# Compact keys and queries, 64-row score products, float32r halves for part of the softmax weights, float32r token transposes

## The chip, the cores and the metric

The kernel runs on one core of one Trainium2 chip. The metric is device time in microseconds (us) of one execution: the median of several runs. A profiled execution gives the trace. In the profile PE is TensorE's matmul queue, PEld its weight loads, DVE VectorE, ACT ScalarE, POOL GpSimd, SP SyncE, which issues most DMAs.

## What is computed

Attention with capped scores over 8 batches, 12 heads, 448 tokens and a head size of 64, and behind it a mixture of 8 experts over the 3584 tokens (model width 768, hidden width 1024):

```python
scores = scale * np.matmul(q, k.transpose(0, 1, 3, 2))
scores = cap * np.tanh(scores / cap)
attn = np.exp(scores - np.max(scores, axis=-1, keepdims=True))
attn = attn / (np.sum(attn, axis=-1, keepdims=True) + 1e-09)
attn_out = np.matmul(attn, v)                 # heads side by side: x, [3584, 768]
...
logits = x @ w_gate + modality_bias[modality_id]
e_idx = np.argmax(logits, axis=1)             # one expert per token
h = np.maximum(x[mask] @ w1[e], 0.0)
out[mask] = gate_w[mask, None] * (h @ w2[e])
```

All inputs and outputs are float32. A product in float32 takes two TensorE instructions, each with its own weight load. float32r is a four-byte type that TensorE multiplies in one instruction; since it keeps fewer bits, the kernel splits a float32 tensor into a float32r high part (a cast) and a float32r rest (a subtract), and adds the products high x high, high x low and low x high.

## The kernel before

**Attention** (`attention`, line 420) runs over 48 head pairs g, two heads j of one batch each, in four steps a pair. Keys lie in units of 128: three of each head (units 0 to 5), and a seventh unit that holds the last 64 keys of both heads. `prep` (line 491), called in step 1 for the next pair, loads keys and queries (`load_qk`, line 383; each head's 64 rows stand twice, in rows 0 to 63 and 64 to 127) and splits them: `kh` is the high part of the keys; `qs` holds the queries' high part in its upper 64 rows and the rest in its lower 64, so that one product over 128 rows with `kh` gives high x high plus high x low; `kl` is the keys' rest. `scores` (line 532) computes two units a step, one in the last: two products of 448 queries for a unit, three for the seventh, into PSUM tile `sc` (line 547); then ACT takes the tanh (line 552) and the exponential (line 553), which gives the softmax weights `pt`, with keys on the rows and queries on the columns.

`weigh` (line 555) runs one pair later: step c multiplies 112 queries of the pair before (the columns of `pt` as stationary weights) with the values `va` as moving columns, 64 values, 8 gate logits and a column of ones a head (73), all in float32: one product for the seventh unit of both heads (line 558, 146 columns) and six of 73 (line 567). After every second step `normalize` (line 575) divides `po` by the column of sums on DVE. In each step PE's order is: the scores of pair g, then the weighing of pair g - 1. The values' gate columns come from small products (`later_gate`, line 461, and `gate_values`, line 395, for the first three pairs, whose line 403 is the only place where outputs of 64 columns are written to halves of the array).

**Experts** (`run_slots`, line 836): slots of 384 tokens of one expert, then shorter ones of 256 or 128 (`ENDS`). A slot gathers its tokens into `xg` (line 716), turns 128 x 128 blocks with TensorE transposes (line 752), splits them, multiplies with `w1` (lines 776 to 780) and `w2` (line 802), each as three float32r products, and scatters the rows. The weights pass through a ring of `nstage` = 4 raw buffers (`load_raw`, line 723, on SP's queue) and are split by ACT (line 732) and DVE (line 733). Short slots use 256 or 512 moving columns for the high weights (line 779) and 128 or 256 for the low ones (line 780).

Of the kernel before, what the change touches and what calls it, by code (L numbers as in the profile page):

```python
# [28 lines left out]
F32 = mybir.dt.float32  # L30
F32R = mybir.dt.float32r
# [3 lines left out]
ALU = mybir.AluOpType  # L35
# [8 lines left out]
VA = D + E + 1  # L44
KU, KR = 3, 64
NU = 2 * KU + 2
KW = 2 * S + KR
OWN = KU * 128
GE = 2 * E
# [15 lines left out]
class Program:  # L65
    def __init__(self, tc, qT, kT, v, vT, cap, mod, wgb, mb, w1, w2, out):
        self.tc, self.nc = tc, tc.nc
        self.qT, self.kT, self.v, self.vT = qT, kT, v, vT
        self.cap, self.mod, self.wgb, self.mb = cap, mod, wgb, mb
        self.w1, self.w2, self.out = w1, w2, out  # L70
# [17 lines left out]
    def constants(self, cpool, dram):  # L88
# [6 lines left out]
        make_identity(nc, self.ident)  # L95
        self.capt = cpool.tile([128, 1], F32, name="capt")
# [286 lines left out]
    def load_qk(self, pool, g, parts=1):  # L383
        nc = self.nc
        b, hp = divmod(g, NP)
        kr = pool.tile([128, 2, S], F32, name="kr")
        qr = pool.tile([128, 2, S], F32, name="qr")
        step = 2 * S // parts
        for i in range(parts):
            cs = slice(i * step, (i + 1) * step)  # L390
            for t, src in ((kr, self.kT), (qr, self.qT)):
                self.load(t.rearrange("p j s -> p (j s)")[:, cs], src[b, hp][:, cs])
        return kr, qr
# [26 lines left out]
    def attention(self, qk, first):  # L420
        tc, nc = self.tc, self.nc
        with ExitStack() as st:
# [11 lines left out]
            khs, kls, kds = [], [], []  # L434
            for i in range(2):
                kh = kp.tile([128, KW], F32R, name=f"kh{i}")
                kl = kp.tile([128, 2, OWN], F32R, name=f"kl{i}")
                kd = kp.tile([128, 2, KR], F32R, name=f"kd{i}")
                nc.gpsimd.memset(kh.bitcast(F32)[:, S : S + KR], 0.0)
                nc.gpsimd.memset(kd.bitcast(F32), 0.0)  # L440
                khs.append(kh)
                kls.append(kl)
                kds.append(kd)
# [47 lines left out]
            def prep(g):  # L491
                b, hp = divmod(g, NP)
                kr, qr = first if g == 0 else self.load_qk(qk, g)
# [3 lines left out]
                kh, kl, kd = khs[g % 2], kls[g % 2], kds[g % 2]  # L497
                qs = sp.tile([128, 2, S], F32R, name="qs")
                qd = sp.tile([128, S], F32R, name="qd")
                keep = self.pin if g < 2 else (lambda inst: inst)  # L500

                copy = (lambda out, in_: keep(nc.scalar.copy(out, in_) if g == 0 else nc.vector.tensor_copy(out, in_)))
                for jj in ((0, 1),) if g else ((0,), (1,)):
                    js = slice(jj[0], jj[-1] + 1)
                    for j in jj:
                        o = j * (S + KR)
                        keep(nc.vector.tensor_copy(kh[:, o : o + S], kr[:, j]))
                    copy(qs[:, js], qr[:, js])
                    keep(nc.vector.tensor_tensor(qs[D:, js], qr[D:, js], qs[D:, js], op=ALU.subtract))  # L509
                    for j in jj:  # L510
                        o, r = j * (S + KR + KR), j * KR
                        keep(nc.vector.tensor_tensor(kl[:, j], kr[:, j, r : r + OWN], kh[:, o : o + OWN], op=ALU.subtract))
                for j in range(2):
                    rows = slice(j * D, (j + 1) * D)
                    r, o = OWN * (1 - j), (OWN, S + KR)[j]
                    copy(qd[rows], qr[rows, j])
                    keep(nc.vector.tensor_tensor(
                        kd[rows, j], kr[rows, j, r : r + KR], kh[rows, o : o + KR], op=ALU.subtract
                    ))
                return qs, qd, kh, kl, kd, va  # L520

            def gate_of(g, va, vt=None):
# [5 lines left out]
                self.put_gate_values(va, vg)  # L528

            GROUPS = ((0, 1), (2, 3), (4, 5), (6,))  # L530

            def scores(step, pt, qs, qd, kh, kl, kd):
                units = GROUPS[step]
                sc = ps_s.tile([128, 2, 512], F32, name="sc")
                for i, u in enumerate(units):
                    if u < 2 * KU:
                        j, c = divmod(u, KU)
                        o = j * (S + 2 * KR) + c * 128
                        todo = [(kh[:, o : o + 128], qs[:, j]), (kl[:, j, c * 128 : (c + 1) * 128], qs[:, j])]
                    else:  # L540
                        todo = [
                            (kh[:, OWN : OWN + 128], qs[:, 0]),
                            (kh[:, S : S + 128], qs[:, 1]),
                            (kd.rearrange("p j s -> p (j s)"), qd),
                        ]
                    for n, (k, q) in enumerate(todo):
                        move = nc.tensor.matmul(sc[:, i, :S], k, q, start=n == 0, stop=n == len(todo) - 1)  # L547
# [3 lines left out]
                n = len(units)  # L551
# [523 lines left out]
```

## Time and profile before

| | us |
|---|---|
| time before, median of 3 runs (lowest to highest) | 1001.65 (1001.46 to 1002.1) |
| the profiled execution's own time | 1003.47 |
| its span, first to last instruction | 1001.9 |
| mean granted TensorE clock | 0.992 of full speed |
| attention, about | 0 to 475 |
| experts, about | 475 to 1002 |

A row of the timeline reads: start, length, engine, line, operation, out<-in, shapes, count; instructions of one kind that follow each other are merged into a row, whose length is from the first start to the last end. A row of a group reads: line, engine, operation, out<-in, shapes, count, then busy us and the mean ns of one, then idle time before them. `128*112 128x73` is a product with stationary weights of 128 rows and 112 columns and 73 moving columns. The trace names float32r operands of TensorE f32 as well.

### The profile page before, as it was taken

What the parts mean: (1) busy time and instruction counts of PE and PEld (TensorE: products, weight loads), DVE (VectorE), ACT (ScalarE), POOL (GpSimd) and SP (SyncE); (2) the same over time, 40 slices, a digit from 0 to 9 for tenths busy, and PEclk for the clock granted to TensorE, in tenths of its full rate; (3) what the DMA queues carried; (4) which work ended last, traced back from release to release, by engine and by line L of the source; (5) the groups of instructions that cost most, each with busy time, mean ns of one, the idle gap of its engine ahead of it and who ended that gap; (6) DMA issues with size and microseconds to landing.
All of it is one profiled execution on the core that took longest, in us unless ns stands there. A gap on an engine that the chain in (4) does not pass through costs nothing. (4 is left out here: it accounts for less than half of the span.)

```text
span 1001.9 us, 17725 instructions
## 1 busy us (share of the span) xinstructions
PE 976.2 (97%) x6628; PEld 941.6 (94%) x6628; DVE 628.6 (63%) x1632; ACT 586.5 (59%) x762; POOL 132.9 (13%) x150
## 2 busy tenths in 40 slices
PE   6999999999999999998999999999999999999996
PEld 4999999999999989997999999999999999998996
DVE  5788888878888688767854444343434344337763
ACT  4678778777778777787254434443434344335552
POOL 2001011020202002022242020202020202001100
PEclk8999999999999999998999999999999999999999
DMA  5555556566555647576386353635353545447750
GB/s 177 154 202 147 201 200 168 179 142 213 167 192 156 200 162 184 178 169 237 73 302 220 126 200 121 211 128 193 134 177 141 181 141 180 142 139 227 253 169 36
DMA packets 61160, 173.38 MB, mean 173 GB/s; under 512 B 10366, under 2 KB 17278, under 8 KB 61056
## 3 DMA queue, kind: packets, MB, share of 16 engines
q1 hardware_dynamic: 51968, 138.97, 44.2%
q0 software_dynamic: 8944, 33.10, 10.0%
q8 instruction: 56, 0.92, 0.4%
q14 instruction: 48, 0.39, 0.1%
q10 hardware_dynamic: 144, 0.00, 0.0%
HBM read 150.52 MB, written 22.69 MB: 173 GB/s over the span
## 5 line engine op out<-in xcount | busy, mean ns | idle before, releaser
L567 PE MATMUL po<-va,pt 128*112 128x73 f32 x2304 | 254.6, 260 | 0.0
L567 PEld LDWEIGHTS po<-va,pt 128*112 128x112 f32 x2304 | 249.9, 179 | 0.2
L552 ACT ACTIVATE th<-sc,isc 128x896 f32<-128x896 f32 x192 | 175.2, 913 | 100.3 <-PE sc L547 99.5
L553 ACT ACTIVATE pt<-th,cabs 128x896 f32<-128x896 f32 x192 | 181.7, 950 | 5.8
L780 PE MATMUL ph<-x,al 128*128 128x384 f32 (+2 forms) x528 | 166.3, 315 | 0.0
L802 PE MATMUL py<-bh,hh 128*128 128x384 f32 x464 | 159.3, 343 | 1.1 <-ACT hh L786 1.1
L547 PE MATMUL sc<-qs,kh 128*128 128x448 f32 x384 | 152.2, 416 | 7.6 <-DVE qs L509 7.6
L802 PE MATMUL py<-bh,hl 128*128 128x384 f32 x464 | 156.1, 336 | 0.0
L802 PE MATMUL py<-bl,hh 128*128 128x384 f32 x464 | 155.4, 335 | 0.0
L776 PE MATMUL ph<-x,ah 128*128 128x384 f32 x384 | 128.5, 335 | 0.7 <-DVE x L759 0.7
L777 PE MATMUL ph<-x,ah 128*128 128x384 f32 x384 | 128.6, 335 | 0.0
L733 DVE TENSOR_TENSOR bl<-raw,bh 128x768 fp32r<-128x768 f32 x88 | 81.2, 955 | 51.0 <-ACT bh L732 49.9
L547 PE MATMUL sc<-qs,kl 128*128 128x448 f32 x288 | 109.3, 380 | 0.1
L732 ACT CAST bh<-raw 128x768 fp32r<-128x768 f32 x88 | 70.4, 840 | 55.9 <-DMA raw<-in_w_dram 51.4
L780 PEld LDWEIGHTS ph<-x,al 128*128 128x128 f32 x528 | 99.5, 188 | 0.0
L807 ACT ACTIVATE ot<-py,mt 128x384 f32<-128x384 f32 x58 | 33.6, 580 | 103.2 <-PE py L802 55.2
L762 DVE TENSOR_TENSOR x<-ptr,x 128x384 fp32r<-128x384 f32 (+2 forms) x66 | 32.6, 518 | 96.8 <-ACT x L761 96.6
L733 DVE TENSOR_TENSOR al<-raw,ah 128x1024 fp32r<-128x1024 f32 x66 | 78.8, 1222 | 17.4 <-ACT ah L732 17.1
L802 PEld LDWEIGHTS py<-bh,hh 128*128 128x128 f32 x464 | 87.3, 188 | 1.5 <-ACT hh L786 1.4
L802 PEld LDWEIGHTS py<-bl,hh 128*128 128x128 f32 x464 | 87.3, 188 | 0.0
L802 PEld LDWEIGHTS py<-bh,hl 128*128 128x128 f32 x464 | 87.1, 188 | 0.1
L786 ACT ACTIVATE hh<-ph 128x384 fp32r<-128x384 f32 x64 | 30.6, 489 | 94.7 <-PE ph L780 94.7
(167 smaller groups left out, 1397.0 us busy)
## 6 DMA issues: line engine op xcount, KB each, us to landing
raw<-in_w_dram SPq DMA_DIRECT2D x66, 512.0 KB, 4.6
raw<-in_w_dram SPq DMA_DIRECT2D x88, 384.0 KB, 4.8
kr<-in_kT_dram SPq DMA_DIRECT2D x47, 448.0 KB, 3.4
qr<-in_qT_dram SPq DMA_DIRECT2D x47, 448.0 KB, 4.5
va<-in_v_dram SPq DMA_DIRECT2D x48, 292.0 KB, 3.7
vt<-in_vT_dram SPq DMA_DIRECT2D x48, 224.0 KB, 4.1
xd<-xs POOLq DMA_DIRECT2D x16, 672.0 KB, 5.4
mapd<-pay,pos POOLq DMA_INDIRECT x32, 5.3
```

What stands on the lines that cost most here:

```text
L547: move = nc.tensor.matmul(sc[:, i, :S], k, q, start=n == 0, stop=n == len(todo) - 1)
L552: nc.scalar.activation(th[:, :n], sc[:, :n, :S], AF.Tanh, scale=self.isc)
L553: nc.scalar.activation(pt[:, units[0] : units[0] + n], th[:, :n], AF.Exp, scale=self.cabs)
L567: nc.tensor.matmul(po[:CP, o0 + j * VA : o0 + (j + 1) * VA], pt[:, j * KU + i, qs_], va[:, 2 * i + j], start=False, stop=j == 1 and i == K ...
L732: a = self.nc.scalar.copy(hi, raw)
L733: b = self.nc.vector.tensor_tensor(lo, raw, hi, op=ALU.subtract)
L762: nc.vector.tensor_tensor(lo, pt[:, :w], hi, op=ALU.subtract)
L776: nc.tensor.matmul(ph[:, :w], hi[:, fs], self.x[:, k, 0, :w], start=first, stop=False)
L777: nc.tensor.matmul(ph[:, :w], hi[:, fs], self.x[:, k, 1, :w], start=False, stop=False)
L780: nc.tensor.matmul(ph[:, :w], lo[:, fs], self.x[:, k, 0, :w], start=False, stop=last)
L802: nc.tensor.matmul(py[:, :HALF], self.h[a][:, f, rows], self.w2s[f][c][:, cs], start=i == 0, stop=i == 3 * FC - 1,)
L807: nc.scalar.mul(ot[:, cs], py[:, :HALF], mt[:, t, 1:2])
```

## The change

Keys and queries come as one tensor `kq` of 960 columns: 384 own keys, two blocks of 64 for the last keys (a head's own block filled, the other zero), 448 queries; head 0 in rows 0 to 63, head 1 in rows 64 to 127, each once. `prep` splits all of it with one cast and one subtract. In steps 0 to 2 `scores` computes the two heads' units as products over 64 rows, three for each head (high x high, low x high, high x low), the heads alternating; step 3 has three products over 128 rows for the shared unit. Units are numbered so that a step's two units are the same keys' block of both heads.

The softmax weights of the first two steps (four of the seven units) are split into float32r halves `ph` and `pl`: the exponential is written in place to `th`, a copy (ACT in step 0, DVE in step 1) gives `ph`, a DVE subtract `pl`. `gate_of` splits the values of these units into `vh` and `vl`. `weigh` uses three float32r products for each of the four units and float32 for the other three; values have 74 columns (one more), and 128 columns of weights are taken instead of 112, out of tiles widened by 16 zero columns. Tokens are gathered into a float32r `xg` and transposed as float32r. `nstage` is 3 instead of 4, `lg` has one buffer instead of two. Setup and the branch for large caps (not run here) follow the new layout.

```diff
-VA = D + E + 1
+VA = D + E + 2
+SPL = 2
+SW = S + 16
+KC2 = OWN + 2 * KR
+QK = KC2 + S
...
+        self.identr = cpool.tile([128, 128], F32R, name="identr")
+        nc.vector.tensor_copy(self.identr, self.ident)
...
+    def load_kq(self, pool, g, parts=1):
+        b, hp = divmod(g, NP)
+        kq = pool.tile([128, QK], F32, name="kq")
+        for cs in (slice(0, QK),) if parts == 1 else (slice(0, KC2), slice(KC2, QK)):
+            self.load(kq[:, cs], self.kq[b, hp][:, cs])
+        return kq
...
+                pts.append(kp.tile([128, NU - 1 - 2 * SPL, SW], F32, name=f"pt{i}"))
+                phs.append(kp.tile([128, 2 * SPL, SW], F32R, name=f"ph{i}"))
+                pls.append(kp.tile([128, 2 * SPL, SW], F32R, name=f"pl{i}"))
+                for t in (pts[i], phs[i].bitcast(F32), pls[i].bitcast(F32)):
+                    nc.gpsimd.memset(t[:, :, S:], 0.0)
...
+                hi = sp.tile([128, QK], F32R, name="hi")
+                lo = sp.tile([128, QK], F32R, name="lo")
...
+                for cs in (slice(0, QK),) if g else (slice(0, KC2), slice(KC2, QK)):
+                    copy = nc.scalar.copy if cs.start else nc.vector.tensor_copy
+                    keep(copy(hi[:, cs], kq[:, cs]))
+                    keep(nc.vector.tensor_tensor(lo[:, cs], kq[:, cs], hi[:, cs], op=ALU.subtract))
+                return hi, lo, va
...
                 self.put_gate_values(va, vg)
+                vh = sp.tile([128, 2 * SPL, VA], F32R, name="vah", bufs=3)
+                vl = sp.tile([128, 2 * SPL, VA], F32R, name="val", bufs=3)
+                nc.vector.tensor_copy(vh, va[:, : 2 * SPL])
+                nc.vector.tensor_tensor(vl, va[:, : 2 * SPL], vh, op=ALU.subtract)
+                return vh, vl, va
+
+            def scores(step, pt, hi, lo):
                 sc = ps_s.tile([128, 2, 512], F32, name="sc")
-                for i, u in enumerate(units):
...
-                    for n, (k, q) in enumerate(todo):
-                        move = nc.tensor.matmul(sc[:, i, :S], k, q, start=n == 0, stop=n == len(todo) - 1)
+                ks = slice(step * 128, (step + 1) * 128)
+                n = 2 if step < KU else 1
+                for i, (k, q) in enumerate(((hi, hi), (lo, hi), (hi, lo))):
+                    for j in range(n):
+                        rows = slice(j * D, (j + 1) * D) if step < KU else slice(0, 128)
+                        move = nc.tensor.matmul(
+                            sc[:, j, :S], k[rows, ks], q[rows, KC2:], start=i == 0, stop=i == 2
+                        )
...
                 nc.scalar.activation(th[:, :n], sc[:, :n, :S], AF.Tanh, scale=self.isc)
-                nc.scalar.activation(pt[:, units[0] : units[0] + n], th[:, :n], AF.Exp, scale=self.cabs)
+                pt, ph, pl = pt
+                if step >= SPL:
+                    u = 2 * (step - SPL)
+                    nc.scalar.activation(pt[:, u : u + n, :S], th[:, :n], AF.Exp, scale=self.cabs)
+                    return
+                us = slice(2 * step, 2 * step + 2)
+                nc.scalar.activation(th, th, AF.Exp, scale=self.cabs)
+                copy = nc.scalar.copy if step == 0 else nc.vector.tensor_copy
+                copy(ph[:, us, :S], th)
+                nc.vector.tensor_tensor(pl[:, us, :S], th, ph[:, us, :S], op=ALU.subtract)
 
             def weigh(step, po, pt, va):
+                (pt, ph, pl), (vh, vl, va) = pt, va
                 o0 = (step % 2) * 2 * VA
-                qs_ = slice(step * CP, (step + 1) * CP)
...
+                qs_ = slice(step * CP, step * CP + 128)
+                todo = [(pt[:, 2 * (KU - SPL), qs_], va[:, 2 * KU :].rearrange("p u d -> p (u d)"), 0, 2 * VA)]
+                for u in range(2 * KU):
+                    o = (u % 2) * VA
+                    if u < 2 * SPL:
+                        todo += [(a[:, u, qs_], c[:, u], o, VA) for a, c in ((ph, vh), (ph, vl), (pl, vh))]
+                    else:
+                        todo.append((pt[:, u - 2 * SPL, qs_], va[:, u], o, VA))
+                for i, (a, c, o, n) in enumerate(todo):
+                    nc.tensor.matmul(po[:, o0 + o : o0 + o + n], a, c, start=i == 0, stop=i == len(todo) - 1)
...
-                        lg = xp.tile([CP, C, H, E], F32, name="lg")
-                    pt = pp.tile([128, 2 * KU + 1, S], F32, name="pt")
+                        lg = xp.tile([CP, C, H, E], F32, name="lg", bufs=1)
+                    pt = pts[g % 2], phs[g % 2], pls[g % 2]
...
-        self.xg = wp.tile([128, TW, DM], F32, name="xg")
+        self.xg = wp.tile([128, TW, DM], F32R, name="xg")
...
             move = nc.tensor.transpose(
-                pt[:, t * 128 : (t + 1) * 128], self.xg[:, t, k * 128 : (k + 1) * 128], self.ident
+                pt.bitcast(F32R)[:, t * 128 : (t + 1) * 128], self.xg[:, t, k * 128 : (k + 1) * 128], self.identr
             )
...
-            self.nstage = 4
+            self.nstage = 3
```

More of the change, by code (lines that the diff above doesn't have):

```diff
@@ L492, in prep @@
                 b, hp = divmod(g, NP)
-                kr, qr = first if g == 0 else self.load_qk(qk, g)
+                kq = first if g == 0 else self.load_kq(qk, g)
                 va = ld.tile([128, NU, VA], F32, name="va", bufs=3)
                 self.load(va.rearrange("p u d -> p (u d)"), self.v[b, hp])
-                kh, kl, kd = khs[g % 2], kls[g % 2], kds[g % 2]
-                qs = sp.tile([128, 2, S], F32R, name="qs")
-                qd = sp.tile([128, S], F32R, name="qd")
+                hi = sp.tile([128, QK], F32R, name="hi")
+                lo = sp.tile([128, QK], F32R, name="lo")
                 keep = self.pin if g < 2 else (lambda inst: inst)
[L502 to L520, printed above, removed]
+                for cs in (slice(0, QK),) if g else (slice(0, KC2), slice(KC2, QK)):
[3 more added lines that the diff above has]
+                return hi, lo, va
             def gate_of(g, va, vt=None):
@@ L558, in weigh @@
-                nc.tensor.matmul(
-                    po[:CP, o0 : o0 + 2 * VA],
-                    pt[:, 2 * KU, qs_],
-                    va[:, 2 * KU :].rearrange("p u d -> p (u d)"),
-                    start=True,
-                    stop=False,
-                )
-                for j in range(2):
-                    for i in range(KU):
-                        nc.tensor.matmul(
-                            po[:CP, o0 + j * VA : o0 + (j + 1) * VA],
-                            pt[:, j * KU + i, qs_],
-                            va[:, 2 * i + j],
-                            start=False,
-                            stop=j == 1 and i == KU - 1,
-                        )
+                qs_ = slice(step * CP, step * CP + 128)
@@ L620, in attention @@
                     if g < NG:
-                        scores(step, pt, *cur[:5])
+                        scores(step, pt, *cur[:2])
                     if step == 1 and g + 1 < NG:
@@ L889, in general @@
                     qt = gp.tile([D, 2, S], F32, name="gq")
[L890 to L892 removed]
                     kt = gp.tile([D, 2, S], F32, name="gk")
[L894 to L896 removed]
+                    for j in range(2):
+                        rows = slice(j * D, (j + 1) * D)
+                        last = slice(OWN + j * KR, OWN + (j + 1) * KR)
+                        for dst, cs in (
+                            (qt[:, j], slice(KC2, QK)), (kt[:, j, :OWN], slice(0, OWN)), (kt[:, j, OWN:], last)
+                        ):
+                            nc.sync.dma_start(dst, self.kq[ds(b, 1), hp, rows, cs].rearrange("o d s -> (o d) s"))
                     vt = gp.tile([128, S], F32, name="gvt")
@@ L905, in general @@
                         h = 2 * hp + j
-                        offs = [KU * 128 if j == 0 else 0] + [(0 if j == 0 else 128) + i * 128 for i in range(KU)]
-                        zero = slice(S, S + KR) if j == 0 else slice(0, KR)
-                        keys = slice(0, S) if j == 0 else slice(KR, S + KR)
+                        offs = [OWN] + [i * 128 for i in range(KU)]
+                        zero = slice(OWN + (1 - j) * KR, OWN + (2 - j) * KR)
+                        last = slice(OWN + j * KR, OWN + (j + 1) * KR)
                         for qc in range(C):
@@ L1011, in layout @@
     q, k, v = (np.asarray(inputs[n]) for n in ("q", "k", "v"))
-    def columns(a):
-        a = np.moveaxis(a.reshape(B, NP, 2, S, D), 4, 2).reshape(B, NP, 1, D, 2 * S)
-        return np.broadcast_to(a, (B, NP, 2, D, 2 * S)).reshape(B, NP, 128, 2 * S).copy()
     last, own = slice(S - KR, S), slice(0, S - KR)
-    qs = q.reshape(B, H, CP, C, D).transpose(0, 1, 3, 2, 4).reshape(B, H, S, D)
-    ks = k.copy()
-    ks[:, 1::2, :KR], ks[:, 1::2, KR:] = k[:, 1::2, last], k[:, 1::2, own]
+    qs = q.reshape(B, H, CP, C, D).transpose(0, 1, 3, 2, 4).reshape(B, NP, 2, S, D)
+    ks = k.reshape(B, NP, 2, S, D)
+    kq = np.zeros((B, NP, 2, D, QK), q.dtype)
+    kq[..., :OWN] = ks[..., own, :].swapaxes(-1, -2)
+    for j in range(2):
+        kq[:, :, j, :, OWN + j * KR : OWN + (j + 1) * KR] = ks[:, :, j, last].swapaxes(-1, -2)
+    kq[..., KC2:] = qs.swapaxes(-1, -2)
     vp = v.reshape(B, NP, 2, S, D)
```

63 lines of the change are left out of this document (12 added, 51 removed).

## The prediction

> **What bounds the kernel now.** I read the page's busy shares first, then one long window of the attention stage, then its timeline step by step.
>
> ```profile
> span 1001.9 us, 17725 instructions
> ...
> PE 976.2 (97%) x6628; PEld 941.6 (94%) x6628; DVE 628.6 (63%) x1632; ACT 586.5 (59%) x762; POOL 132.9 (13%) x150
> ```
>
> TensorE (PE) is busy 97% of the span. The page says that matmul ends are modelled, so I go by distances between starts.
>
> ```profile
> 50.00:450.00 400.00, 398.10 (x3160) 379.58 (x3159) 325.22 (x1065) 316.12 (x347) 46.14 (x48) 1.00 0.59 179
> ```
>
> ```profile
> L581 DVE TENSOR_TENSOR xs<-po,rec 112x256 f32<-112x256 f32 x84 | 35.0, 417 | 0.7
> ```
>
> In this window of attention (columns after the length: PE, weight load, VectorE, ScalarE, POOL, granted clock, DMA share, GB/s) line 581 ran 84 times, twice a head pair: 42 pairs in 400 us, **9.52 us a pair**, of which PE is busy 9.48, VectorE (DVE) 325.2/42 = 7.74, ScalarE (ACT) 316.1/42 = 7.53. PE sets the pace; the other two have 1.8 and 2.0 us of room.
>
> ```profile
> 305.37 0.67 PE L547 MATMUL sc<-qs,kh 128*128 128x448 f32 x2
> 305.88 0.37 PE L547 MATMUL sc<-qd,kd 128*128 128x448 f32 x1
> 306.08 0.41 PE L558 MATMUL po<-va,pt 128*112 128x146 f32 x2
> ...
> 307.44 0.45 PE L547 MATMUL sc<-qs,kh 128*128 128x448 f32 x1
> 307.73 0.37 PE L547 MATMUL sc<-qs,kl 128*128 128x448 f32 x1
> ...
> 308.34 0.41 PE L558 MATMUL po<-va,pt 128*112 128x146 f32 x2
> 308.59 1.31 PE L567 MATMUL po<-va,pt 128*112 128x73 f32 x12
> 309.70 0.45 PE L547 MATMUL sc<-qs,kh 128*128 128x448 f32 x1
> ```
>
> One step is 307.44 to 309.70, 2.26 us. Its four float32r score products start 0.205 apart (307.73 to 308.34 is three of them), but the first 0.29 before the second: 0.08 more for the turn from f32 to float32r. Scores take 0.90 (307.44 to 308.34), weighing the values 1.36 (308.34 to 309.70). The fourth step has three score products, 0.71 (305.37 to 306.08). So a pair is 3 x 0.90 + 0.71 + 4 x 1.36 = 8.85, and 0.67 goes to gate products and the rest. An f32 matmul is two instructions, each with its own weight load: a weigh is 2 of 146 columns at 0.125 (308.34 to 308.59 for both) and 12 of 73.
>
> ```profile
> L567 PEld LDWEIGHTS po<-va,pt 128*112 128x112 f32 x2304 | 249.9, 179 | 0.2
> 304.35 1.06 PEld L567 LDWEIGHTS po<-va,pt 128*112 128x112 f32 x10
> 28.60 0.52 PEld L403 LDWEIGHTS vg<-wgt,vt 128*128 128x128 f32 x4
> ```
>
> Ten weight loads of 112 columns take 1.06: (1.06 - 0.18)/9 = 0.098 each. Four of 128 columns, with only 16 moving ones (line 403): (0.52 - 0.19)/3 = 0.11. So **the weigh is paced by loading weights**, at 0.86 ns a column, not by its 73 moving columns. Built up it would be 2 x 0.125 + 12 x 0.098 = 1.43; measured 1.36, since its first loads run ahead: minus 0.07.
>
> **Weighing, after.** Per step two f32 instructions stay for the unit of both heads (148 columns), four for units 4 and 5 in place of eight, and four units turn into twelve float32r products of 74 columns. All weights have 128 columns instead of 112. Twelve products replace eight instructions, so everything hangs on what one costs. The nearest rows are float32r with 128-column weights in the last, 128-token slot of the expert stage:
>
> ```profile
> 982.51 0.34 PE L779 MATMUL ph<-x,ah 128*128 128x256 f32 x1
> 982.68 0.22 PE L780 MATMUL ph<-x,al 128*128 128x128 f32 x1
> 982.74 0.33 PE L779 MATMUL ph<-x,ah 128*128 128x256 f32 x1
> ```
>
> ```profile
> 982.56 0.19 PEld L780 LDWEIGHTS ph<-x,al 128*128 128x128 f32 x1
> 982.69 0.19 PEld L779 LDWEIGHTS ph<-x,ah 128*128 128x128 f32 x1
> 982.79 0.19 PEld L780 LDWEIGHTS ph<-x,al 128*128 128x128 f32 x1
> 982.91 0.19 PEld L779 LDWEIGHTS ph<-x,ah 128*128 128x128 f32 x1
> ```
>
> Two products of 256 and 128 columns come every 0.23 (982.51 to 982.74), though at the 0.205/448 = 0.46 ns a column of the score products they would stream in 0.176. Their loads start 0.10 to 0.13 apart. I read this as two loads of about 0.11 in a row: float32r weights load no faster than f32 ones. I take **0.11 a product**. Bounds: 0.034 if only 74 columns streamed, 0.06 as the shortest distance that I see (982.68 to 982.74), 0.13 as the longest distance of loads. The weigh is then 2 x 0.125 + 0.08 (turn to float32r) + 12 x 0.11 + 4 x 0.11 - 0.07 = 2.02, +0.66 a step. There are 48 x 4 = 192 weighs: **+127 us** (at 0.034: -48; at 0.06: +12; at 0.13: +173).
>
> The Trainium skill, "TensorE: Matmul & The Clock Gate", section "Weight-path perf modes", speaks for the change here: fast weight load comes on when there are 128 weights and the type is not FP32, and padding to 128 columns meets that; the same table sees no win for fp32, four bytes like float32r. The four-byte 128-column loads above do not show it; with it the sum would be that of the fast-load rival below.
>
> **Scores, after.** Steps 0 to 2 issue six products of 64 rows instead of four of 128, heads alternating: rows 0-63 and 64-127, a PSUM bank each. No row shows half-row products. The nearest are half-column ones of line 403, in the first pairs only:
>
> ```profile
> 28.85 0.49 PE L403 MATMUL vg<-wgt,vt 128*128 128x16 f32 x3
> 29.27 0.29 PE L403 MATMUL vg<-wgt,vt 128*64 128x16 f32 x4
> 29.49 0.38 PE L558 MATMUL po<-va,pt 128*112 128x146 f32 x1
> L403 PE MATMUL vg<-wgt,vt 128*64 128x16 f32 x12 | 0.9, 220 | 0.0
> ```
>
> Four products on two 64-column halves start within 0.29 - 0.22 = 0.07; at 0.86 ns a column their four loads in a row would take 0.22. So halves do run side by side. The turn costs: three full-width products 0.11 apart put the last at 29.07, and the first half-width one starts 0.20 later instead of 0.11; from the last (29.34) to the next full one (29.49) 0.15 pass. I take 0.10 for each turn, one in and one out a step, the turn in covering that to float32r. Bounds for the six products: three at 0.205 (pairs side by side) to six at 0.205. I take pairs at two loads, 0.22: 3 x 0.22 + 0.20 = 0.86 instead of 0.90, and 144 such steps give **-6 us** (bounds: -0.20 a step, -29 us, to the serial rival). Step 3 keeps three full products: 0.
>
> **What lies beside PE.**
>
> ```profile
> L509 DVE TENSOR_TENSOR qs<-qr,qs 64x896 fp32r<-64x896 f32 x42 | 45.8, 1089 | 1.1
> L512 DVE TENSOR_TENSOR kl<-kr,kh 128x384 fp32r<-128x384 f32 x83 | 44.6, 551 | 0.0
> L502 DVE CAST qd<-qr 64x448 fp32r<-64x448 f32 x84 | 32.5, 387 | 1.2
> L507 DVE CAST kh<-kr 128x448 fp32r<-128x448 f32 x82 | 30.5, 399 | 18.1 <-DMA kr<-in_kT_dram 17.7
> L502 DVE CAST qs<-qr 128x896 fp32r<-128x896 f32 x41 | 25.7, 627 | 5.0 <-DMA qr<-in_qT_dram 5.0
> L517 DVE TENSOR_TENSOR kd<-kr,kh 64x64 fp32r<-64x64 f32 x84 | 18.2, 216 | 0.4
> L553 ACT ACTIVATE pt<-th,cabs 128x896 f32<-128x896 f32 x127 | 132.7, 1045 | 4.1
> L732 ACT CAST bh<-raw 128x768 fp32r<-128x768 f32 x88 | 70.4, 840 | 55.9 <-DMA raw<-in_w_dram 51.4
> ```
>
> DVE loses, a pair, 1.09 + 0.63 + two each of 0.551, 0.387, 0.399 and 0.216: 4.82. It gains (subtracts at 1.05 ns a column, casts at 0.53, from these rows) cast and subtract of 960 columns (0.66 + 1.16), of 296 value columns (0.31 + 0.46), one cast of 896 weights (0.63) and two subtracts (2 x 1.09): 5.40. So 7.74 becomes 8.32. ACT gains one copy of 896, about 0.95: 8.48. A pair on PE becomes 4 x 2.02 + 3 x 0.86 + 0.71 + 0.67 = 12.04, which hides both: 0. The new subtracts add waits on DVE, for ACT's exponential and copy; queued behind them are the normalizing of `po` (two buffers, so PE waits for it only two half-pairs later) and the next pair's casts, and DVE has 12.04 - 8.32 = 3.7 us a pair to absorb that: 0. Were PE to fall under 8.5, ACT would bound.
>
> **The other edits.** Keys and queries of a pair are one 480 KB load instead of two of 448 KB, hidden by PE in the stream: 0. Only the first pair is waited for: 416 KB less at 179 GB/s (the long window above) is 2.3 us at most, part of it taken by subtracts before the first lo product; I take -1.5 (0 to -2.3).
>
> ```profile
> 474.50 0.82 PE L752 MATMUL ptr<-ident,xg 128*128 128x128 f32 x6
> 46.39 0.49 PE L483 MATMUL vgp<-ident,vgs 96*128 96x96 f32 x4
> 950.00:1002.00 52.00, 43.38 (x280) 41.72 (x278) 26.44 (x57) 20.58 (x38) 2.97 (x3) 0.97 0.33 106
> ```
>
> Token transposes come every (0.82 - 0.27)/5 = 0.11 (0.27 is the mean length of one), with 96 moving columns and the same 128 loaded (line 483, one lasts 0.25) every (0.49 - 0.25)/3 = 0.08: paced by moving columns, at twice float32r's time. float32r lies between 0.06 (128 x 0.46 ns) and 0.11; I take 0.08, the lowest that a row shows for such a load: 180 x -0.03 = **-5 us** (-9 to 0). With three raw weight buffers instead of four, SP's queue, which also carries the attention's loads, issues a raw load when the split three loads back has read its buffer, not four back. The short last slots have the least room: PE is busy 43.4 of the last 52 us and idles 8.6. Bounds 0 and another 8.6; I take +1, near the lower end, since three buffers still load ahead.
>
> **Sum.** +127 - 6 - 1.5 - 5 + 1 = +115.5. The profiled execution took 1003.5 (span 1001.9 and 1.6 around it): 1119. It lies 1.8 above the median of the runs, 1001.65, so I predict **1117**.
>
> **Rivals.** *Serial half-rows.* If the 64-row products do not overlap, a step's scores are 6 x 0.205 + 0.20 = 1.43, 0.57 over my 0.86; 144 steps add 82: **1199**. For it: every full-row product in the rows starts one at a time. Against: the half-column products.
>
> *Fast load: faster than before.* If float32r weights of 128 columns load in 0.034 or less, the twelve products stream: weigh 2 x 0.125 + 0.08 + 12 x 0.034 + 0.44 - 0.07 = 1.11, a pair on PE 8.4, and ACT's 8.48 becomes the floor. With some waiting between the two engines, 8.6 a pair: 48 x -0.92 = -44, and -5.5 from the rest: **952** (945 to 990). It decides from 0.06 a product: 0.70 + 12 x 0.06 = 1.42, +0.06 x 192 = +12 against -11.5. For it: the full-width transposes of line 483 load 128 four-byte columns in 0.08, so 0.11 is no floor of the port. Against: the loads at 982.56 to 982.91, float32r like the new ones.
>
> **Chances.** Forecast 0.50; serial 0.20; fast load 0.22; a product between 0.06 and 0.10 (1010 to 1085) 0.08. The likeliest case alone spans 1085 to 1160 (0.13 a product at the top; -29 from scores and 0.10 a product at the bottom). For 8 in 10 the range runs from 985 to 1215: it leaves out most of the fast-load case and a tail above. About 0.2% is what a measurement of this kernel tells from no change: faster 0.22, same 0.03, slower 0.75.
>
> **What will show it.** Loads of the weigh 0.11 apart and each weigh near 2.0 confirm the main term; under 0.06 apart it is wrong, and ACT should then be almost without idle time. The two products of a score pair starting together confirm -6, 0.2 apart the serial rival. A pair of 12.0 us moves the end of attention from about 475 to 595; DVE and ACT should then idle a third of it.

## The result: 1319.6 us instead of 1001.6

The changed kernel takes **1319.6 us** (median of four runs: three from 1319.02 to 1319.66, and one of 1379.78, which the ratio leaves out) beside 1001.56 us for the kernel before (1000.24 to 1002.1): a ratio of 1.3176, with an interval of 1.315 to 1.3202. The forecast was 1117 with a range up to 1215, so the direction was right and the size was not. The profiled execution took 1319.66, with a span of 1317.9.

The page of the changed kernel, cut to its span, the busy shares and the granted clock by slices:

```profile
span 1317.9 us, 19766 instructions
...
PE 1288.9 (98%) x7684; PEld 1190.2 (90%) x7684; DVE 676.9 (51%) x1492; ACT 631.1 (48%) x807; POOL 126.0 (10%) x152
...
PEclk7555589759899588995555899999999999999998
```

TensorE is still the engine that is always busy, and the two others have more room than before. The new thing is the last line: a digit of 5 is a slice of 33 us in which the throttle, which sets the clock of TensorE, granted half of full speed. They all lie in the first 24 slices, the attention stage.

One step at full clock, from the timeline:

```profile
404.23 0.47 PE L529 MATMUL sc<-hi 64*128 64x448 f32 x2
404.54 0.36 PE L529 MATMUL sc<-hi,lo 64*128 64x448 f32 x2
404.74 0.37 PE L529 MATMUL sc<-lo,hi 64*128 64x448 f32 x2
405.04 0.52 PE L559 MATMUL po<-va,pt 128*128 128x148 f32 x2
405.30 0.29 PE L559 MATMUL po<-vah,ph 128*128 128x74 f32 x1
...
406.54 0.28 PE L559 MATMUL po<-vah,pl 128*128 128x74 f32 x1
406.65 0.65 PE L559 MATMUL po<-va,pt 128*128 128x74 f32 x4
407.23 0.47 PE L529 MATMUL sc<-hi 64*128 64x448 f32 x2
```

The step lasts 3.00 us (404.23 to 407.23), 0.81 of it scores and 2.19 weighing. The two 64-row products of a pair are merged into one row, x2: they start together. Twelve float32r products follow, 405.30 to 406.54 for eleven distances, so 0.11 each.

The same step at half clock (the rows between are left out):

```profile
113.44 0.74 PE L529 MATMUL sc<-hi 64*128 64x448 f32 x2
...
115.59 0.41 PE L559 MATMUL po<-val,ph 128*128 128x74 f32 x1
115.80 0.41 PE L559 MATMUL po<-vah,pl 128*128 128x74 f32 x1
...
118.98 0.74 PE L529 MATMUL sc<-hi 64*128 64x448 f32 x2
```

It lasts 5.54 us, and the products come 0.21 apart. Two stretches of the changed kernel side by side (length, then PE busy with its count, granted clock, DMA share, GB/s):

```profile
20.00:160.00 140.00, 140.00 (x604) 0.50 0.18 57
350.00:400.00 50.00, 49.64 (x393) 1.00 0.30 97
```

Busy time doesn't tell them apart, PE is full in both. The count does: 4.3 instructions a us in the first, 7.9 in the second. Read in one-microsecond windows, the granted clock in attention is at half for **406 us** in seven spells (stretches at half clock): 16 to 173, 245 to 296, 340 to 350, 422 to 473, 518 to 528, 600 to 719, 729 to 736. Before, it was low there for 14 us in all. In the experts' part it is low for another 12 us, where it was 3 before.

Attention ends at 797.4 (the first full product of `w1`) instead of 483.6, +314; the experts behind it take 520 instead of 518. All but 2 us of the loss is attention.

### The profile page after: what moved, and what is told of

The parts are those of the page before. It is cut to its first block, busy times and chain, and to the rows that moved or that the text cites. A ratio compares the mean times of both kernels' runs of the same rounds, so it can differ in the third digit from the quotient of the medians.

```text
span 1317.9 us, 19766 instructions
## 1 busy us (share of the span) xinstructions
PE 1288.9 (98%) x7684; PEld 1190.2 (90%) x7684; DVE 676.9 (51%) x1492; ACT 631.1 (48%) x807; POOL 126.0 (10%) x152
## 5 line engine op out<-in xcount | busy, mean ns | idle before, releaser
L559 PE MATMUL po<-va,pt 128*128 128x74 f32 (+1 forms) x1152 | 268.6, 353 | 0.3 <-ACT pt L539 0.3
L559 PE MATMUL po<-vah,ph 128*128 128x74 f32 x768 | 254.9, 332 | 0.0
L559 PEld LDWEIGHTS po<-va,pt 128*128 128x128 f32 x1152 | 213.8, 241 | 44.2 <-issue 36.2
L559 PE MATMUL po<-val,ph 128*128 128x74 f32 x768 | 251.5, 328 | 0.0
L559 PE MATMUL po<-vah,pl 128*128 128x74 f32 x768 | 251.2, 327 | 0.0
L559 PEld LDWEIGHTS po<-val,ph 128*128 128x128 f32 x768 | 186.6, 243 | 5.2 <-issue 5.1
L559 PEld LDWEIGHTS po<-vah,ph 128*128 128x128 f32 x768 | 186.3, 243 | 0.5 <-issue 0.5
L559 PEld LDWEIGHTS po<-vah,pl 128*128 128x128 f32 x768 | 186.5, 243 | 0.0
L545 DVE TENSOR_TENSOR pl<-th,ph 128x896 fp32r<-128x896 f32 x96 | 104.0, 1083 | 52.8 <-ACT ph L544 52.8
L529 PE MATMUL sc<-hi 64*128 64x448 f32 (+1 forms) x336 | 109.4, 571 | 4.5 <-DVE hi L504 4.5
```

What stands on the lines that cost most here:

```text
L529: move = nc.tensor.matmul(sc[:, j, :S], k[rows, ks], q[rows, KC2:], start=i == 0, stop=i == 2)
L545: nc.vector.tensor_tensor(pl[:, us, :S], th, ph[:, us, :S], op=ALU.subtract)
L559: nc.tensor.matmul(po[:, o0 + o : o0 + o + n], a, c, start=i == 0, stop=i == len(todo) - 1)
```

## The experiments

Each is an edit of the changed kernel, or of the one before where it says so. Half-clock time is counted as above. A "gap" is idle time of PE. The "streaming share" in the expectations is an estimate: the moving columns of a step, those of each f32 instruction counted twice (the f32 transposes of line 483 take 0.08 us for 96 columns, 0.86 ns a column), times the time of a column, over the length of the step. At the 0.205/448 = 0.46 ns that the score products show it is 84% (before), 62% (full rows) and 52% (changed kernel). The 76, 56 and 47 of the expectations go by a shorter time a column, which no run shows; their order is the same.

**1. The scores alone** (`e1_scores`): the new layout, the 64-row products and the float32r transposes, with the old f32 weighing and a ring of four.

```diff
-                        todo += [(a[:, u, qs_], c[:, u], o, VA) for a, c in ((ph, vh), (ph, vl), (pl, vh))]
...
+                    nc.tensor.matmul(
+                        po[:CP, o0 + o : o0 + o + VA], pt[:, u, qs_], va[:, u], start=False, stop=u == 2 * KU - 1
+                    )
```

> The change without its new weighing: float32 weights of 112 columns for all seven units as before, ring of four, but compact keys, 64-row score products and float32r transposes. Theory 'empty array' (the clock falls because the load-paced weighing streams columns for only a part of its time): the clock stays at 0.98 or more, a step takes 0.81 + 1.36 = 2.17 us instead of 2.26, 144 such steps give 13 us and the transposes 3: 980 to 990 us. Theory 'half rows' (the clock falls because 64-row products use half of the array): spells at half clock in attention, over 1050 us. Theory 'gap' (the wait of the rank products for VectorE alone trips it): no statement on the scores, clock as before if PE has no such gap.

Measured: 1032.28 us (1025.76 to 1036.6), ratio 1.0324 [1.0288, 1.036]: slower by itself. Its timeline:

```profile
300.27 0.47 PE L516 MATMUL sc<-hi 64*128 64x448 f32 x2
...
301.07 0.50 PE L528 MATMUL po<-va,pt 128*112 128x146 f32 x2
...
302.65 0.47 PE L516 MATMUL sc<-hi 64*128 64x448 f32 x2
...
303.94 0.41 PE L528 MATMUL po<-va,pt 128*112 128x146 f32 x2
...
305.30 0.45 PE L516 MATMUL sc<-hi 128*128 128x448 f32 x1
```

Scores take 0.80, 0.10 less than before. But the weighing between two half-row steps takes 1.58 (301.07 to 302.65), against 1.36 before it and 1.36 here ahead of the full-row step (303.94 to 305.30). So the turns into and out of half rows cost 0.22 that does not lie inside the scores. The step is 2.38 instead of 2.26: +0.12 in 144 steps, +17 us, where the forecast had -6. The rest of the 31 us includes 7.6 us of waits for gate products and 10 us more of half clock; I did not divide it further.

**2. Full-row scores** (`e2_fullrows`): the new weighing with four products over 128 rows, as many as before. Each of them then sums the rows of both heads, so the scores are not those of one head and tokens go to other experts; TensorE's work in attention is of the old size.

```diff
-                        rows = slice(j * D, (j + 1) * D) if step < KU else slice(0, 128)
+                parts = ((hi, hi), (lo, hi), (hi, lo))[: 2 if step < KU else 3]
...
+                            sc[:, j, :S], k[:, ks], q[:, KC2:], start=i == 0, stop=i == len(parts) - 1
```

> The change with the four 128-row score products a step of before in place of six of 64 rows, new weighing kept. Each product sums both heads' rows, so the output is not the reference's, tokens go to other experts and only the attention stage is compared. 'Empty array': the half-clock spells stay, mean clock of attention under 0.9, a step 0.90 + 2.19 = 3.1 us where the clock is full. 'Half rows': full clock from about 30 us on, attention ends near 620 us instead of 793.

Measured: 1116.63 (one execution). Timeline, and the clock line of its page:

```profile
303.64 0.45 PE L529 MATMUL sc<-hi 128*128 128x448 f32 x1
...
304.53 0.41 PE L559 MATMUL po<-va,pt 128*128 128x148 f32 x2
...
306.49 0.45 PE L529 MATMUL sc<-hi 128*128 128x448 f32 x1
```

```profile
PEclk8999999999999999999999999999999999999999
```

Weighing takes 1.96 (2.02 was forecast) where before it took 1.36, and 0.60 x 192 = 115 us is all of the difference to 1001.6. **The weighing is as slow as forecast, and it alone does not lower the clock**: 14 us at half, at the start. The step is 2.85; the changed kernel's 3.00 is 0.15 more, in 144 steps 22 us, which agrees with experiment 1.

**3. More columns to stream** (`e4_wide`): each float32r product takes 148 columns instead of 74, half of them not used; the first f32 product of a step takes 222 instead of 148.

```diff
-                        todo += [(a[:, u, qs_], c[:, u], o, VA) for a, c in ((ph, vh), (ph, vl), (pl, vh))]
...
+                            (a[:, u, qs_], c[:, u : u + 1].to_broadcast([128, 2, VA]), two)
```

> The change, but each float32r product of the weighing streams its 74 value columns twice (the copy goes to PSUM columns that nobody reads), and the first f32 product 222 columns instead of 148; same number of weight loads. It only adds work: about 0.12 us a step for the first product, 23 us in all. 'Empty array': the clock stays full for most of attention and the total falls to 1130 to 1180 us, some 150 us under the changed kernel. 'Half rows' and 'gap': no less than 1300 us.

Measured: 1235.12 (1229.09 to 1236.88), ratio 1.2329 [1.2285, 1.2373]. Twice the columns in the weighing, and 85 us faster than the changed kernel, though not as fast as expected. Half clock is 123 us in nine spells of 7 to 17 us, although its gaps are larger:

```profile
PE rank L227 <- DVE oh L218: 8.3, 7, 1.2
PE vgp L485 <- DVE vgs L481: 16.6, 14, 1.2
```

(Rows of the waits: who waits for what, us in total, times, the longest.) A spell begins within 3 us of each of the seven gaps of 1.2 us ahead of the rank products, and with more streaming the spells are short. But the fourteen gaps of the second row, 0.9 to 1.2 us long and ahead of the small products of line 485 behind the gate products, start none. So the length of a gap alone does not decide.

**4. Weights of 112 columns** (`e5_pad112`): the padding to 128 taken back.

```diff
-                qs_ = slice(step * CP, step * CP + 128)
+                qs_ = slice(step * CP, (step + 1) * CP)
...
-                    nc.tensor.matmul(po[:, o0 + o : o0 + o + n], a, c, start=i == 0, stop=i == len(todo) - 1)
+                    nc.tensor.matmul(po[:CP, o0 + o : o0 + o + n], a, c, start=i == 0, stop=i == len(todo) - 1)
```

> The change with 112 columns of weights in the weighing, as before, instead of 128: 16 of its loads shrink from 0.11 to 0.098, 0.19 us a step, 36 us in all at full clock. The stream share rises from 0.47 to about 0.51: fewer or shorter spells, 1150 to 1285 us. If 128 columns were loaded faster than 112, as the padding seems meant, it is slower than the changed kernel's 1320.

```profile
202.37 0.27 PE L559 MATMUL po<-vah,ph 128*112 128x74 f32 x1
...
203.16 0.27 PE L559 MATMUL po<-vah,pl 128*112 128x74 f32 x1
```

Eight distances in 0.79, 0.099 a product against 0.111 with 128 columns: 0.87 to 0.88 ns a column in both. Padding buys no faster load; it costs an eighth. The time was 1240.65 and 1277.98 in two executions, both below the changed kernel.

**5 and 6. Serial half rows** (`e8_serial`, and `e10_serialpin` with that order held): all three products of head 0 ahead of those of head 1.

```diff
-                for i, (k, q) in enumerate(((hi, hi), (lo, hi), (hi, lo))):
-                    for j in range(n):
+                for j in range(n):
+                    for i, (k, q) in enumerate(((hi, hi), (lo, hi), (hi, lo))):
```

> The change with the score products of a step ordered head by head, so that neighbours use the same half of the rows and cannot run side by side: scores of 6 x 0.205 and two turns, about 1.4 us instead of 0.81, +0.6 a step, 144 steps: 85 us at full clock. If the clock follows the share of time in which columns stream, that share rises from 0.47 to about 0.55, spells are as rare as in e2_fullrows and the total is 1200 to 1230 us. If half rows count half, the share is about 0.40 and attention runs at half clock nearly throughout: over 1400 us.

> As e8_serial, whose score products ran in the changed kernel's order all the same, now with that order pinned: the three products of head 0 on rows 0-63, then those of head 1 on rows 64-127. Scores and turns take 1.4 us instead of 0.8, +0.6 a step, 85 us at full clock. If the clock follows the share of time in which columns stream, whatever the rows, the share is 0.55 as in e2_fullrows, spells are rare or short and the total is 1220 to 1260 us. If half rows count half, the share is about 0.40, attention runs at half clock nearly throughout: over 1450 us.

Measured: 1307.97 and 1224.02 (one execution each). Neither priced what it was made for. The timeline of the second, first a usual step, then one whose first product ran alone, behind a wait (in brackets the idle time before a row and what ended it):

```profile
451.45 0.48 PE L529 MATMUL sc<-hi 64*128 64x448 f32 x2
...
451.96 0.37 PE L529 MATMUL sc<-lo,hi 64*128 64x448 f32 x2
```

```profile
19.81 0.71 PE L529 MATMUL sc<-hi 64*128 64x448 f32 x1 [3.31 <-DVE hi L504]
...
21.67 0.74 PE L529 MATMUL sc<-hi,lo 64*128 64x448 f32 x1
21.68 0.74 PE L529 MATMUL sc<-hi 64*128 64x448 f32 x1
```

Three products of rows 0 to 63 come first in the program, and still each starts together with its counterpart on rows 64 to 127. The second fence shows that the order was held: there the first half is one product ahead, and the other half's first product (21.68) starts beside its second one, ahead of its third. The two halves advance independently of the order, so a serial version is not to be had in this way. The full-clock steps are alike; the times differ from 1320 since the spells do (266 and 171 us, and at the start, from 20 to 130 and from 20 to 43, products at half-clock distances under a recorded clock of 1.00; see experiment 7).

**7 and 8. Taking gaps away** (`e3_norank`, `e9_nogap`). In the changed kernel the first spell begins inside a gap of 3.9 us at setup (14.4 to 18.4), and each later one begins up to 3 us after a gap of 0.78. The first of these, in the timeline:

```profile
242.03 0.18 PE L227 MATMUL rank<-oh,tri 112*112 112x32 bf16 x1 [0.78 <-DVE oh L218]
...
244.55 0.38 PE L559 MATMUL po<-vah,ph 128*128 128x74 f32 x1
244.74 0.41 PE L559 MATMUL po<-val,ph 128*128 128x74 f32 x1
244.95 0.41 PE L559 MATMUL po<-vah,pl 128*128 128x74 f32 x1
```

PE stands 0.78 us for the routing of a finished batch, a chain of small DVE operations (line 218), works 2.5 us at 0.11 a product, and then at 0.21. The waits of before and after at this product, and the one of after at setup:

```profile
PE rank L218 <- DVE oh L209: 0.3, 1, 0.3
```

```profile
PE rank L227 <- DVE oh L218: 4.7, 6, 0.8
PE sc L529 <- DVE hi L504: 4.5, 2, 3.9
```

The first edit issues the rank products two steps later; the second also defers the early count of the tokens.

```diff
+                    if step == 2 and late is not None:
+                        late()
+                        late = None
...
-                        self.route(pb, plg, rp, self.ps_r)
+                        late = self.route(pb, plg, rp, self.ps_r)
```

> The change with the two rank products of the routing (and what follows them) issued two steps of the next pair later, when VectorE has their operand. 'Gap': no fall of the clock after the first rise, so of 406 us at half clock only the first 160 stay: about 1195 us. 'Empty array': the gap is only what trips a stage that is near the limit; spells become fewer, but the clock still takes as long to rise, 1195 to 1319 us, and any other gap of half a microsecond trips it.

> As e3_norank, and the early count of tokens (its product waited 1.08 us for VectorE and stood right before the one spell of 123 us left there) two steps later too. 'Gap trips, low stream share holds': no spell after the first rise, mean clock 0.98 or more, 1150 to 1185 us. If the clock falls at a stage of this kind without a gap, the spells come back at other places and the time stays above 1200.

Measured: 1222.96 (two executions) for the first; 1158.02 and 1181.48 for the second, whose trace is of 1158.02. In the first the falls behind the rank products are gone, and one is left, 583 to 706, behind a gap of another kind:

```profile
582.02 0.17 PE L270 MATMUL cps<-acc,ones 112*128 112x8 bf16 x1 [1.08 <-DVE acc L224]
```

The second takes that one away too, and only 601 to 639 is left, behind a gap of 0.94 at 599. **These gaps of 0.8 to 1.1 us start the spells**: moved away, they take the spells behind them along. That is so for these places, not for every gap of the length, as experiment 3 showed. One more spell was hard to see: in the first 105 us of `e3_norank` the page shows a granted clock of 1.00, but the products come at half-clock distances (45 instructions in 90 to 100, 42 in 105 to 110). The record of the clock seems to begin only with the first change; distances tell more. In `e9_nogap` it is so from 20 to 40.

**9 to 11. The same gap in three kernels** (`e13_halfgap` from experiment 8, `e11_fullgap` from experiment 2, `e12_beforegap` from the kernel before): in one step of every sixth pair PE waits for four small DVE copies of a score tile.

```diff
+                        for _ in range(4):
+                            nc.vector.tensor_copy(gap, sc[:CP, 0, :64])
...
+                        self.pin(nc.tensor.matmul(idle[:CP, :64], self.tri, gap, start=True, stop=True))
```

> The kernel of e9 (changed kernel, rank products and early count deferred; 1158 to 1181 us), with one forced PE gap a batch: in step 0 of every sixth pair a chain of four small copies of a score tile on DVE ends in a small product that stands between the scores and the weighing in PE's order. Theory, a gap trips the clock and the low streaming share keeps it low: most of the eight gaps, if they last 0.7 us or more, are followed by a half-clock spell of 10 to 150 us; time 1220 to 1330. Rival, the spells came from the rank products' own place at the end of a batch and not from a gap as such: no spell behind these gaps, time about 1170.

> The kernel of e2 (full-row score products, 1116.6 us, streaming share 56%; each score product sums both heads' rows), with the same forced gap as e13 and so eight gaps of the same kind. Theory, gap and streaming share decide whatever the rows: gaps of 0.7 us or more trip the clock here too, with spells of 7 to 25 us as in e4 at 61%; time 1130 to 1180. Rival, products over half the rows count as half the activity and only they bring the long spells: no spell behind the gaps, time 1120 to 1130.

> The kernel before with the same forced gap as e13 and e11 (streaming share 76%). Theory, share decides: no spell behind the gaps, or spells below 8 us; time 1005 to 1030. If gaps alone decided, each would be followed by a spell of tens of us and the time would pass 1050.

| one execution each | forced gaps, us in total | half clock, us | time | without the gaps |
|---|---|---|---|---|
| half-row scores, new weighing | 22.1 in eight | 584 | 1427.65 | 1158.02 |
| full-row scores, new weighing | 14.9 in seven, 2.9 ahead of a gate product | 276 | 1259.79 | 1116.63 |
| before | 48.9 in eight | 65 | 1067.16 | 1001.56 |

The copies waited their turn on DVE, so the gaps are longer than meant, up to 10.5 us in the kernel before; that is one reason why all three times lie above what was expected, and longer spells are the other. The comparison holds all the more: with the longest gaps, the kernel before has the shortest spells. Its windows around one gap, and those of `e11_fullgap`:

```profile
105.00:110.00 5.00, 0.34 (x2) 0.91 0.76 111
110.00:115.00 5.00, 4.88 (x21) 0.50 0.55 182
115.00:120.00 5.00, 5.00 (x40) 0.90 0.01 5
```

```profile
400.00:405.00 5.00, 4.27 (x21) 0.64 0.34 120
430.00:435.00 5.00, 5.00 (x20) 0.50 0.00 0
455.00:460.00 5.00, 5.00 (x41) 0.90 0.00 0
```

The kernel before is back at full clock 4 to 7 us after the gap. In the full-row kernel the spells behind its eight gaps last 3 to 55 us (27, 3, 55, 7, 55, 7, 55, 34); three more of 7 us (from 296, 477 and 657) begin about 1 us after rank products that had waited only 0.46. In the half-row kernel the spells last 58 or 102 us behind seven of eight gaps and 89 behind the last. The rival, that only products over half the rows bring long spells, falls: `e11_fullgap` has no such products, and spells of 55 us. My theory falls in its simple form too, since with a streaming share of 56% I expected 7 to 25 us: the share does not give the length.

**12. What ends a spell** (`e14_dense`). In the changed kernel all seven recorded spells end at one kind of place. The second, in the timeline:

```profile
293.65 0.58 PE L529 MATMUL sc<-lo,hi 64*128 64x448 f32 x2
294.15 0.69 PE L475 MATMUL vga<-vh,wg 128*96 128x448 f32 x1
294.64 0.57 PE L476 MATMUL vga<-vl,wg 128*96 128x448 f32 x1
...
295.57 0.38 PE L559 MATMUL po<-val,ph 128*128 128x74 f32 x1
295.79 0.28 PE L559 MATMUL po<-vah,pl 128*128 128x74 f32 x1
295.90 0.28 PE L559 MATMUL po<-vah,ph 128*128 128x74 f32 x1
```

Two gate products of 448 columns directly behind the scores make the longest dense run of a pair, and about 1 us behind it the products come faster again. So it is at 171, 348, 471, 526, 717 and 734, and at seven of eight ends in `e13_halfgap`. Not every such run ends a spell (there is one a pair). The edit makes it longer:

```diff
                         later_gate(g + HB - (step == 0), vts.pop(0))
+                        if g > 1:
...
+                            for _ in range(6):
+                                nc.tensor.matmul(more[:, :S], cur[0][:, :128], cur[0][:, KC2:], start=True, stop=True)
```

> The changed kernel with 264 products added: once a pair, beside the two gate products that follow the scores of step 2, six more float32r products of 448 columns over 128 rows, whose result is not used. At the full clock they cost 264 x 0.205 = 54 us, so a sum of work alone gives 1320 + 54 = 1374 or more. Theory: a half-clock spell ends only where the array streams columns without a pause for long enough, and in the changed kernel the only such place is the scores of step 2 with the two gate products behind them (all seven spells of its attention end there); with the run made longer each spell ends at the first or second such place, within 10 to 30 us instead of up to 157. Then about 330 us of half clock go, which cost 45 to 50% of their length: 1374 - 150 = about 1225, with the same gaps and the same falls. Rival, the spells end by themselves after some time, or by chance: 1374 to 1440, spells as long as before.

Measured: **1230.96** (1222.54 and 1239.37), ratio 1.2307 [1.2102, 1.2511]; 258 products were added. Waits and clock of the longer of the two executions:

```profile
PE rank L227 <- DVE oh L218: 5.5, 7, 0.8
```

```profile
PEclk7589899998998998998989999999999999999999
```

The seven gaps of 0.8 are all still there, and behind six of them the clock still falls (not behind the one at 215); the spells are now 7 to 10 us, but for the one from the start, which ends at 72, just behind the first of the added runs (69.3). In all 102 us instead of 406. More work made the kernel 89 us faster.

**13. The transposes alone** (`e6_transposes`): the kernel before with float32r token transposes.

```diff
-        self.xg = wp.tile([128, TW, DM], F32, name="xg")
+        self.xg = wp.tile([128, TW, DM], F32R, name="xg")
...
-                pt[:, t * 128 : (t + 1) * 128], self.xg[:, t, k * 128 : (k + 1) * 128], self.ident
+                pt.bitcast(F32R)[:, t * 128 : (t + 1) * 128], self.xg[:, t, k * 128 : (k + 1) * 128], self.identr
```

> The kernel before with float32r token transposes alone. Spacing falls from 0.11 to 0.09 as in the changed kernel: 180 x 0.02 = 3.6 us, 996 to 999 us; nothing else moves. It would be the fastest kernel of the study.

Measured: **996.07** (12 runs, 993.92 to 1000.01), ratio 0.9953 [0.9936, 0.997]. Beside 1000.39 for the kernel before in the same session that is 4.3 us, small but clear of the noise. It is the one part that pays, and this version beats both kernels. In the changed kernel the transposes look so:

```profile
787.67 0.68 PE L739 MATMUL ptr<-identr,xg 128*128 128x128 f32 x6
```

With 0.24 for one, (0.68 - 0.24)/5 = 0.09 a transpose instead of 0.11, and in other groups 0.08; 180 times 0.02 to 0.03 is 3.6 to 5.4 us, in which the 4.3 lie.

## Why the prediction was wrong

**Where the 318 us come from.** Weighing: 115 (experiment 2). Turns of the half-row scores at full clock: 22 (the step of 3.00 against 2.85). That makes 1139. Half clock: a step takes 5.54 instead of 3.00, so each us of it loses 1 - 3.00/5.54 = 0.46 us; (406 - 14) x 0.46 = 180. Sum 317. The same sum gives the other times: 1139 + 53 for the added products + (102 - 14) x 0.46 = 1232 for `e14_dense` (its profiled execution took 1239), for `e8_serial`, with 110 us not recorded, 1139 + (266 + 110 - 14) x 0.46 = 1306 (1308), and for `e13_halfgap`, with 22 us of gaps and 22 us of half clock that is not recorded at the start, 1139 + 22 + (584 + 22 - 14) x 0.46 = 1433 (1428).

**The step that failed** is the one under all the terms: that distances between starts read at a granted clock of 1.00 would hold in the changed kernel. The forecast quotes that 1.00 for the window of before and multiplies from there; its bounds of 0.034 to 0.13 for a product leave out the 0.21 that a third of the run shows. Two things in its own text pointed there. It found that the weighing would be "paced by loading weights", so that twelve products would wait for loads most of the time; and it set the waits of the new DVE work at 0, since DVE has 3.7 us of room a pair. That room is real, but it is a mean. At the end of a batch the routing chain comes late for once, and PE stands 0.78 us six times where before it stood 0.3 once. (In the trace the chain follows the new cast and subtract of 960 columns; that these make it late was not tested by itself.) As idle time that is 4.7 us. As a trigger it brought the six later spells, 249 us at half clock, which cost 249 x 0.46 = 115 of the 180. The other 65 lie in the spell of 157 us that begins in the gap of 3.9 at setup; before, a gap of 1.6 stood there and the spell was 7 us.

**What keeps the clock low.** Shown: the gaps of 0.8 us at the rank products, and the forced ones of 1.8 us and more, start spells; spells end mostly at runs of dense streaming, and lengthening these runs shortens the spells. The kernel before rides over a gap of 1.22 us and falls in one of 3.72, for 7 us (453 to 460); the first stands ahead of the same small products (`vgp`, there line 483) as the fourteen in `e4_wide` that start no spell either. The two gaps in the timeline of before:

```profile
355.05 0.55 PE L483 MATMUL vgp<-ident,vgs 96*128 96x96 f32 x4 [1.22 <-DVE vgs L479]
...
454.34 0.71 PE L547 MATMUL sc<-qs,kh 128*128 128x448 f32 x1 [3.72 <-DVE qs L509]
```

Not shown: the rule. I have no row for what the throttle counts, nor for why one gap starts a spell and a longer one at another product does not, nor for why one dense run ends a spell and the one before it did not.

The Trainium skill, "TensorE: Matmul & The Clock Gate", section "Part 1: The HAM clock gate (the "warmup" mystery)", says that the clock is either half or full and returns after about 3.4 us of sustained work. The trace agrees on the two values, 0.50 and 1.00. It does not agree on the return: with PE busy for 140.00 of 140.00 us the clock stayed at 0.50. The section "HAM oscillation — how this bites in real kernels" of the same page of the Trainium skill warns of idle gaps over about 3.4 us; here 0.78 was enough. The measurement decides: PE's busy time in a profile does not tell whether the clock is kept.

**The other steps.**
- *Weighing, +127:* 0.11 a product was right (0.111), and 1.96 a weigh between full-row steps against 2.02: +115.
- *Scores, -6:* the pairs do run side by side, 0.20 apart, so the serial rival is out. The term that was mis-sized is the turn. I put both at 0.20 a step; measured it is 0.31 - 0.20 at the first pair, 0.30 - 0.20 behind the last, and 2.19 - 1.96 = 0.23 around the weighing, together 0.44. Between +17 and +22 us came instead of -6.
- *Fast load, 952:* refuted by the 0.111 and by experiment 4, which has no faster load from 128 columns.
- *DVE and ACT, 0:* right as a mean. Four pairs in the 50 us from 350, 12.5 a pair where 12.04 was forecast (the turns); DVE is busy for 31.0/4 = 7.8 of it (8.32 was forecast), ACT for 33.7/4 = 8.4 (8.48).
- *Prologue, -1.5:* the first score product starts at 8.15 instead of 10.28. *Transposes, -5:* -4.3 by themselves. *Ring of three, +1:* the experts' part is 2 us longer in spite of the transposes; 9 us more of half clock lie in it too, so how much of this is the ring stays open, as it was not run alone.
- *End of attention at 595:* 601 with full rows at full clock (experiment 2), 797 in the changed kernel.
- *Lower end of the likeliest case, 1085:* the terms named there (0.10 a product, -29 from the scores) give 1117 - 23 - 23 = 1071. Nothing hangs on it, since the result lies above the range.

## What to carry to other kernels

Splitting a float32 product with few moving columns into three float32r products multiplies weight loads, and where loads set the pace it costs what they cost. When a change makes the stream of TensorE thinner, price every new idle gap of it at the clock it may lose, not at its length; look for a dense run that brings the clock back, and compare counts of instructions per us, since busy time looks the same at both clocks. Try the parts one by one: here only the transposes paid.

## What the hardware showed that I had not expected

- A gap of 0.78 us ahead of the rank products halves the clock 0.1 to 3 us later, in a stream limited by weight loads; the low clock then lasted from 7 to 119 us behind such gaps, and 157 us from the start. Fourteen gaps of up to 1.2 us at other products (`e4_wide`) did not halve it.
- Six added dense products a pair (53 us of work) took 304 us of half clock away.
- Products on the two row halves of the array start in pairs even where three products of one half stand ahead of the other's in the program.
- A half-row step costs 0.44 us of turns, more than the whole of what two halves side by side save here.
- Until the first change in a trace the clock is recorded as 1.00, also over stretches of 85 and 110 us in which products came at half-clock distances.
